# Gated linear attention with a bilinear feed-forward: scores of a 128-token block taken by its first and last 64 tokens, and a new order of all steps

## The chip, the cores and the metric

The kernel runs on one core of one Trainium2 chip. The metric is the time of one execution in microseconds on the device; the median of three runs of the kernel before is 193.85 us (193.69 to 193.97). The engines are called as in the profile: PE (TensorE, with its weight loads as PEld), DVE (VectorE), ACT (ScalarE), POOL (GpSimd) and SP (SyncE, which here only issues DMAs).

## The reference

There are 4 batch rows, 8 heads, 768 tokens and a head width of 48. Per batch row and head a 48 x 48 state is decayed row by row, updated and read:

```
for t in range(S):
    state = alpha[:, :, t, :, None] * state + einsum('bhd,bhe->bhde', k[:, :, t], v[:, :, t])
    y[:, :, t] = einsum('bhd,bhde->bhe', q[:, :, t], state)
x = y.transpose(0, 2, 1, 3).reshape(3072, 384)
out = ((x @ w_a) * (x @ w_b)) @ w_out        # w_a, w_b: 384 x 1536, w_out: 1536 x 384
```

## The kernel before

**Tiling.** The work is cut into six chunks, c = 0 to 5. A chunk is two batch rows (u = 0, 1; even c take rows 0 and 1, odd c rows 2 and 3) times 256 tokens. The 256 tokens lie on 128 partitions as pairs (r = 0, 1 within the pair), and the partitions fall into two halves of 64 (g = 0, 1); a half is a block of 128 consecutive tokens. Within a block the recurrence is worked out as masked scores between keys and queries; from block to block it goes through the state.

**The steps of one chunk**, with the short names that the program uses:

- `ld` loads alpha (a), k, q and v; `ln` (L556, ACT) takes logarithms of alpha; `B`, `A2` or `AQ` (PE) form running sums; `E` (L667, ACT) takes exponentials i and b of them; `ra`, `lv` scale one token of each pair; `mk`, `mq` (L678, DVE) write the scaled keys and queries into `QKp`, with heads padded from 48 to 64 columns.
- `C` (L736, PE) transposes `QKp` with eight 128 x 128 transposes per half of the heads, and `Ce` (L742, L744) copies the result from PSUM to `kqT`. That is so for chunks 0 and 1; for chunks 2 to 5 `T` (L767) is a DMA transpose issued by SP.
- `v` (L785, L787) copies the loaded values into `vx`, whose heads are padded with zeros from 48 to 96 columns (`cz .. v P`, L513, a POOL memset).
- `D` (L841, PE) forms scores, one call per u and half h of the heads: 16 matmuls of a 64 x 64 quarter of the array, each with 128 columns (the block's queries, both r). A stationary operand holds the block's 64 keys of one r. The result, 128 x 1024, is masked on its way out of PSUM by DVE (`M`, L846), or copied by ACT (`Mc`, L850) and masked in place by DVE (`Mm`, L854).
- `K` and `K2` (L799, L812, PE) form the state's updates, `k` (L826 to L830, DVE) applies them; `SB`, `SA` (PE, L865) are the parts of the output that come from the state, `Y` (PE, L865) is the part from the scores: 48 quarter matmuls with 128 columns per u. `X` (L900, L902) copies the output to `xT`.
- The feed-forward: `a f w` and `b f w` (L919, PE) are three matmuls each for the 128 columns f of w_a or w_b, with 512 columns of tokens (w = *) or 256 (one u); `as` (L925, ACT) copies a's result, `pr` (L933, DVE) multiplies; `o` (L941) and `oc` (L952) are the last product, `ot` and `otc` (L956, L958) copy it, `st` and `stc` store it (SP; one by ACT).

**The order** is written out by hand in a string `PROGRAM`: each entry is one step with its engine (V is DVE, S is ACT, P is POOL, Y is SP) and its PSUM bank. No planner runs when the kernel is built; each engine takes its instructions in the order of the string and waits for the semaphores of what it reads and overwrites. So an entry has two meanings: its place among the entries of its own engine, and its data. Between engines the string sets nothing. The weight loads `W a lo hi`, `W b lo hi` (L529) and `Wo` (L532) cast from float32 to bf16 and are issued by POOL, among POOL's own work.

PSUM has eight banks; a `D` and a `Y` take two, the other steps one.

Of the kernel before, what the change touches and what calls it, by code (L numbers as in the profile page):

```python
# [82 lines left out]
0: cs 1 0 P; o 3 1 -
1: k 0 0 V; k 0 1 V; Mm 0 0 V; SB 0 1; C 1 0 3; C 1 1 7
0: ot 3 S; o 0 1 -
1: Ce 1 0 V
2: ln *
1: v 1 V; D 1 0 3; Ce 1 1 S; K2 1 1 6 0; Y 0; SA 0
0: ot 0 V
1: k 1 0 V; D 1 1 6  # L90
0: o 2 0 5
1: M 1 0
2: l2 0 V
1: X 0 S; a 3 0 1; Mc 1 1
2: l2s 0 P; l2s 1 P
1: a 2 0 3; a 4 0 4
2: R 0
1: k 1 1 V; as 4 0
2: ra 1
1: as 3 0; b 4 0 7  # L100
0: o 2 1 -
1: as 2 0
0: ot 2 S
1: pr 4 0
2: R 1; lv 1 q P
1: b 3 0 6; b 2 0 7; a 5 0 2; pr 3 0; b 5 0 3; as 5 0; b 1 0 5; a 1 0 1; pr 5 0; pr 2 0; a 7 0 2; as 1 0; pr 1 0
2: AQ 3
1: SB 1 6
2: lv 0 k P
1: a 10 0 5  # L110
2: lv 1 k V; ra 0; ld v * P
1: Mm 1 1 V
2: E 1 b
1: as 10 0; b 10 0 0; pr 10 0
2: mq 1 V; E 1 i
1: as 7 0; b 7 0 1
2: E 0 b; E 0 i
1: a 0 0 5
0: st 3 Y
2: dr  # L120
1: SA 1; Y 1
2: mk 1 V
1: pr 7 0; a 11 0 0; a 6 0 3; b 6 0 2; X 1 S; b 11 0 4; a 2 1 6; as 6 0; a 3 1 7; as 11 0; b 2 1 1; pr 6 0
2: lv 0 q V
1: b 4 1 0; as 2 1
2: T 1
1: pr 11 0
2: dl
0: st 0 Y
1: a 0 1 2; pr 2 1  # L130
2: mq 0 V
1: b 3 1 3; b 0 0 6; as 3 1; as 0 0; b 0 1 7; pr 3 1; a 8 0 1; a 9 0 5
0: st 1 Y
1: b 8 0 3; b 9 0 4; pr 0 0; as 0 1
2: mk 0 V
1: a 4 1 2
3: ln *
1: a 9 1 6; pr 0 1; as 8 0; b 9 1 1
3: ra 1
1: b 10 1 7; pr 8 0; a 10 1 3; as 4 1; as 9 0; as 9 1; a 6 1 6; b 6 1 2; b 11 1 5; pr 4 1; as 10 1; pr 9 0; a 11 1 4; pr 10 1; pr 9 1; as 6 1  # L140
2: v 1 S
1: a 8 1 3; b 8 1 1; a 7 1 6; pr 6 1
3: l2 0 V
1: as 11 1
2: T 0
1: as 8 1; a 5 1 4
3: ra 0
1: as 5 1; a 1 1 2
2: v 0 V
4: ld a * Y  # L150
1: pr 11 1; as 7 1; pr 8 1
2: K2 * * 0 7; D 1 1 3; D 1 0 5
1: as 1 1; b 5 1 2; o 2 0 1
2: k * 0 V
1: pr 5 1
3: v 0 S; v 1 S
1: b 1 1 2
2: Mc 1 0; M 1 1
3: l2s 0 P; l2s 1 P
1: b 7 1 0; o 2 1 -; pr 1 1; o 3 0 4  # L160
2: SB 0 5
1: pr 7 1
3: R 0
2: D 0 0 2
1: ot 2 V
2: Mm 1 0 V
1: o 3 1 -
2: Mc 0 0; SB 1 0; D 0 1 2
3: R 1
1: ot 3 S  # L170
2: SA 0
1: o 0 0 4
0: cs 0 0 P
2: Mc 0 1
4: ln *
3: ld q * Y; ld k * Y
2: k * 1 V
3: AQ 2
2: Y 1; SA 1; Mm 0 1 V; Mm 0 0 V; Y 0; X 0 S
3: E 0 b  # L180
4: l2 0 V
2: X 1 V
1: o 0 1 -
2: b 1 * 6; a 1 * 5
3: E 1 b
4: ld k * Y
3: E 1 i
1: ot 0 S
3: E 0 i
4: l2s 0 P  # L190
2: a 0 * 0; b 0 * 1; as 0 *; as 1 *
3: lv 0 k P; lv 0 q P
2: a 5 * 7
1: st 3 Y
2: a 7 * 4
4: l2s 1 P
2: a 2 * 5
3: lv 1 q V; mq 1 V; lv 1 k V
2: pr 1 *
3: dr  # L200
2: pr 0 *
3: mk 0 V
4: ld q * Y
0: st 2 Y
2: as 5 *; a 6 * 6; b 6 * 2; as 7 *
3: mq 0 V
2: b 9 * 4; b 7 * 0
1: st 2 Y
3: dl
4: R 0  # L210
2: b 5 * 7
1: o 1 0 3
2: a 9 * 1; pr 7 *; as 6 *
3: T 0
2: pr 6 *
4: ra 0
# [188 lines left out]
def kernel(  # L405
# [11 lines left out]
    nc = tc.nc  # L417
# [148 lines left out]
    def bank(i):  # L566
        return psum[:, int(i)]
# [531 lines left out]
```

## Time and profile before

| | |
|---|---|
| median of three runs | 193.85 us |
| the profiled execution, first to last instruction (its span) | 192.0 us |
| that leaves around the span, against the median | 1.85 us |
| PE busy (matmuls as the profile models them) | 186.8 us |
| DVE busy | 133.1 us, 223 instructions |
| ACT busy | 106.5 us, 194 instructions |
| POOL busy | 56.9 us, 75 instructions |
| granted TensorE clock, mean | 1.000 |

The profile is one execution. Its chain of work that ended last is followed back from the last instruction: at each step to what released it, or to the instruction before it on its engine. Its time line lists instructions with their start, their duration and, in brackets, the idle time of the engine before them and what ended it. Matmuls overlap, so the duration of one says less than the distance between the starts of two.

### The profile page before, as it was taken

What the parts mean: (1) busy time and instruction counts of PE and PEld (TensorE: products, weight loads), DVE (VectorE), ACT (ScalarE), POOL (GpSimd) and SP (SyncE); (2) the same over time, 40 slices, a digit from 0 to 9 for tenths busy, and PEclk for the clock granted to TensorE, in tenths of its full rate; (3) what the DMA queues carried; (4) which work ended last, traced back from release to release, by engine and by line L of the source; (5) the groups of instructions that cost most, each with busy time, mean ns of one, the idle gap of its engine ahead of it and who ended that gap; (6) DMA issues with size and microseconds to landing.
All of it is one profiled execution on the core that took longest, in us unless ns stands there. A gap on an engine that the chain in (4) does not pass through costs nothing.

```text
span 192.0 us, 6086 instructions
## 1 busy us (share of the span) xinstructions
PE 186.8 (97%) x2613; PEld 116.9 (61%) x2613; DVE 133.1 (69%) x223; ACT 106.5 (55%) x194; POOL 56.9 (30%) x75
## 2 busy tenths in 40 slices
PE   7999999999999999999999999999999999999992
PEld 3888875677778876645557444656465644545562
DVE  2387698994989888899897956887567446252510
ACT  4448885656779867753487756743572435314211
POOL 8999626752450500640074262000000000000000
PEclk9999999999999999999999999999999999999999
DMA  5999999999969999999999989017641200000422
GB/s 132 274 219 218 251 253 235 244 269 264 251 107 166 165 216 265 248 254 149 233 213 181 156 174 129 3 42 140 146 66 44 85 0 0 0 0 3 164 82 82
DMA packets 62618, 29.40 MB, mean 153 GB/s; under 512 B 53712, under 2 KB 60768, under 8 KB 62592
## 3 DMA queue, kind: packets, MB, share of 16 engines
q0 software_dynamic: 18432, 13.37, 39.6%
q1 hardware_dynamic: 44016, 15.55, 38.1%
q8 instruction: 20, 0.33, 0.7%
q10 hardware_dynamic: 144, 0.10, 0.2%
q14 instruction: 6, 0.05, 0.1%
HBM read 25.98 MB, written 4.74 MB: 160 GB/s over the span
## 4 chain that ended last, share of the span: by engine, by line
PE 91%; DMA 5%; SPq 1%; DVE 1%; issue 1%; ACT 0%; DVEq 0%
PE psum L919 47%; PE psum L941 24%; PE psum L865 7%; PE psum L841 3%; DMA kqT<-QKp 3%; DMA q_t<-in_q_dram 3%; PE psum L736 2%; PE psum L633 1%; PE psum L952 1%; SPq L549 1%; PE psum L799 1%; PE psum L812 1%; PE psum L700 1%; PE psum L591 1%; PE psum L592 1%
## 5 line engine op out<-in xcount | busy, mean ns | idle before, releaser
L919 PE MATMUL psum<-xT,wb_t 128*128 128x512 bf16 (+1 forms) x270 | 56.0, 337 | 0.0
L919 PE MATMUL psum<-xT,wa_t 128*128 128x512 bf16 (+1 forms) x270 | 56.0, 337 | 0.0
L941 PE MATMUL psum<-wo_t,prod 128*128 128x384 bf16 x276 | 49.4, 326 | 0.0
L919 PEld LDWEIGHTS <-wb_t 128*128 128x128 bf16 x270 | 25.9, 98 | 19.9 <-issue 0.5
L919 PEld LDWEIGHTS <-wa_t 128*128 128x128 bf16 x270 | 25.9, 98 | 19.7 <-issue 0.3
L941 PEld LDWEIGHTS <-prod 128*128 128x128 bf16 x276 | 25.9, 98 | 17.6
L956 ACT ACTIVATE ot<-psum 128x384 f32<-128x384 f32 (+1 forms) x16 | 7.7, 482 | 22.7 <-PE psum L941 21.6
L850 ACT ACTIVATE m<-psum 128x1024 bf16<-128x1024 f32 x14 | 14.1, 1023 | 4.6 <-PE psum L841 4.3
L613 POOL TENSOR_TENSOR l<-la 64x384 f32<-64x384 f32 x7 | 7.8, 1108 | 26.6 <-ACT la L556 19.0
L846 DVE TENSOR_TENSOR m<-psum,mask 128x1024 bf16<-128x1024 f32 x10 | 12.1, 1220 | 3.1 <-PE psum L841 3.1
L652 POOL TENSOR_TENSOR q_t<-q_t,ra 128x384 f32<-128x384 f32 x5 | 6.1, 1215 | 22.5 <-ACT ra L645 19.7
L556 ACT ACTIVATE la<-a_t 128x1536 f32<-128x1536 f32 (+2 forms) x9 | 9.5, 1055 | 2.3 <-DMA a_t<-in_alpha_dram 2.2
L678 DVE TENSOR_TENSOR QKp<-q_t,beta 128x768 bf16<-128x768 f32 x10 | 10.0, 995 | 1.0 <-ACT beta L667 1.0
L865 PE MATMUL psum<-m,vx 64*64 64x128 bf16 x576 | 10.5, 217 | 0.0
L900 ACT ACTIVATE xT<-psum 128x768 bf16<-128x768 f32 x9 | 7.2, 816 | 5.7 <-PE psum L865 5.5
L678 DVE TENSOR_TENSOR QKp<-k_t,invb 128x768 bf16<-128x768 f32 x10 | 9.7, 972 | 0.8 <-ACT invb L667 0.8
L854 DVE TENSOR_TENSOR m<-m,mask 128x1024 bf16<-128x1024 bf16 x14 | 9.3, 684 | 1.2 <-ACT m L850 1.2
L958 DVE COPY ot<-psum 128x384 f32<-128x384 f32 (+1 forms) x9 | 4.8, 532 | 7.6 <-PE psum L941 4.7
L865 PEld LDWEIGHTS <-vx 64*64 64x64 bf16 x576 | 9.0, 107 | 0.5 <-issue 0.3
L841 PE MATMUL psum<-kqT 64*64 64x128 bf16 x384 | 9.0, 219 | 0.4 <-DMA kqT<-QKp 0.3
L652 POOL TENSOR_TENSOR k_t<-k_t,a_t 128x384 f32<-128x384 f32 x6 | 7.4, 1228 | 6.1 <-issue 3.3
L549 POOL DMA_DIRECT2D v_t<-in_v_dram x8 | 8.5, 1058 | 0.1
(271 smaller groups left out, 287.9 us busy)
## 6 DMA issues: line engine op xcount, KB each, us to landing
out_dram<-ot SPq DMA_DIRECT2D x23, 192.0 KB, 3.8
q_t<-in_q_dram SPq DMA_DIRECT2D x3, 768.0 KB, 6.5
a_t<-in_alpha_dram POOLq DMA_DIRECT2D x2, 768.0 KB, 15.2
k_t<-in_k_dram POOLq DMA_DIRECT2D x2, 768.0 KB, 12.1
v_t<-in_v_dram POOLq DMA_DIRECT2D x4, 384.0 KB, 7.0
a_t<-in_alpha_dram SPq DMA_DIRECT2D x2, 768.0 KB
k_t<-in_k_dram SPq DMA_DIRECT2D x2, 768.0 KB
a_t<-in_alpha_dram POOLq DMA_DIRECT2D x3, 384.0 KB, 8.5
```

What stands on the lines that cost most here:

```text
L549: eng.dma_start(out=t[:, us, hs].rearrange("p b h r d -> p (b h) (r d)"), in_=src[ch.b0 + us.start:ch.b0 + us.stop, hs, ch.s * 2 * C:(ch.s ...
L556: nc.scalar.activation(out=ch.la[:, us, hs].rearrange("p b h r d -> p (b h r d)"), in_=ch.a[:, us, hs].rearrange("p b h r d -> p (b h r d) ...
L613: eng.tensor_add(ch.l2[(1 - g) * HC:(2 - g) * HC, 1], x[:, :, 0, :], x[:, :, 1, :])
L652: eng.tensor_mul(x, x, by)
L678: eng.tensor_mul(QKp[ch.c % 2][:, u, j, :, hs, :D], src[:, u, hs].rearrange("p h r d -> p r h d"), f)
L841: nc.tensor.matmul(s2[g * HC:(g + 1) * HC, r, p, rk, :], lhsT=turned_part(ch, u, 1, rk, 2 * h + p, g, rs), rhs=queriesT(ch, u, 2 * h + p, ...
L846: nc.vector.tensor_mul(m.rearrange("p r a k s -> p (r a) (k s)"), ch.s2[u, h].rearrange("p r a k s -> p (r a) (k s)"), maskn(4))
L850: nc.scalar.activation(out=m.rearrange("p r a k s -> p (r a) (k s)"), in_=ch.s2[u, h].rearrange("p r a k s -> p (r a) (k s)"), func=AF.Copy)
L854: eng.tensor_mul(x, x, maskn(4))
L865: nc.tensor.matmul(y[c * DP:(c + 1) * DP, g, j // 2 * C:(j // 2 + 1) * C], lhsT=lhsT, rhs=rhs, start=(g, c) not in begun, stop=False, skip ...
L919: nc.tensor.matmul(p, lhsT=(wa_t, wb_t)[w][:, kk, f * 128:(f + 1) * 128], rhs=ch.xT[:, kk, us, :], start=(kk == 0), stop=(kk == KT - 1))
L941: nc.tensor.matmul(op, lhsT=ch.prod[:, f, at:at + C], rhs=wo_t[:, f, :], start=(f == 0), stop=(f == NFF - 1))
```

## The change

A block's 128 tokens were split by r: a stationary operand held the 64 tokens of one r. Now they are split into the first 64 tokens (x = 0) and the last 64 (x = 1). The last 64 keys are read only with the last 64 queries, so their score matmul has 64 columns and not 128, and likewise the `Y` matmul of x = 1. The scores of a call are 128 x 768 and not 128 x 1024, and the mask is 192 columns wide and not 256.

For this the keys of one x must lie together. In chunks 0 and 1 the transposes write PSUM in that order. In chunks 2 to 5, after the DMA transpose, a new step `Tr` copies the key half of `kqT` (128 x 1024, bf16) into a new tile `kp`: eight calls, five on DVE and three on ACT. The values must lie likewise: `v` copies them as before, and a new step `vs` then overwrites two of four quarters of 32 partitions in `vx` with the tokens of the other r (two instructions of 32 partitions x 384 each): 24 calls, 11 on DVE, 6 on ACT, 7 on POOL. `K` and `K2` read the loaded values and no longer `vx`.

The PROGRAM string is new from end to end. The steps of each kind are as many as before. What else stands on other engines than before: `Ce` six on ACT and two on DVE (before two and six), `v` four on ACT and eight on DVE (nine and three), `lv` seven on POOL and 13 on DVE (11 and nine), `l2s` four and four (seven and one), `l2` two on POOL and four on DVE (none and six).

The first lines of the string, before and after (up to the place where the feed-forward begins):

```diff
-0: cm 0; c1; cz 0 b P; ci; ld a 0b Y; c1a; ld a 0a Y; ln 0b; cu; cz 1 b P; fill 7 2; cu2 V; cz 0 q V; cus; ld k 0b Y; ld k 0a Y; B 0b 5; ld q 0b Y; ld v 0 P
-0: ln 0a; ld q 0a Y; E 0b b; E 0b i; mq 0b V; B 0a 0; E 0a i; dk 0 2; E 0a b; ld a 1 P; mk 0b V; C 0 1 5; cs 0 m P; ld k 1 P; ld q 1 P; v 0 S; mk 0a V; cm 1
-0: de 0; fill 2 1; mq 0a V; C 0 0 3; Ce 0 1 V; W b 0 256; cz 0 v P; Ce 0 0 V; D 0 1 4; ln 1; ld v 1 P; W a 256 768; K 0 0 6; k 0 0 V; M 0 1; D 0 0 0; SB 0 6
-0: cz 1 q P; B 1a 2; M 0 0; W a 0 256; E 1a i; E 1a b; W b 256 768; mq 1a V; mk 1a V; B 1b 4; dk 1 3; E 1b i; E 1b b; de 1; v 1 S; mq 1b V; mk 1b V; C 1 0 0
-0: Y 0; SA 0; Ce 1 0 V; cs 1 m P
+0: cm 0; c1; cz 0 b P; ci; ld a 0b Y; c1a; ld a 0a Y; ln 0b; cu; cz 1 b P; fill 7 0; cu2 V; cz 0 q V; cus; ld k 0b Y; ld k 0a Y; B 0b 2; ld q 0b Y
+0: ln 0a; B 0a 0; E 0b i; mk 0b V; ld v 0 P; fill 2 4; E 0b b; mq 0b V; C 0 1 2; ld q 0a Y; E 0a b; mq 0a V; dk 0 3; E 0a i; mk 0a V; ld a 1 P; C 0 0 0; Ce 0 0 V
+0: cs 0 m P; Ce 0 1 S; D 0 1 4; K 0 0 2; D 0 0 0; de 0; ln 1; ld k 1 P; v 0 S; k 0 0 V; SB 0 2; ld q 1 P; cm 1; M 0 0; vs 0 0 S; vs 0 1 P; W b 0 256; M 0 1
+0: B 1a 6; E 1a b; mq 1a V; B 1b 0; dk 1 4; E 1a i; mk 1a V; E 1b b; C 1 0 5; E 1b i; mq 1b V; cz 0 v P; Y 0; ld v 1 P; SA 0; mk 1b V; K 1 1 0; v 1 V
+0: vs 1 0 V; vs 1 1 V; de 1; K 1 0 1; k 1 0 V; C 1 1 4; Ce 1 1 V; Ce 1 0 S; D 1 0 6; X 0 S; W a 256 768; a 3 0 1; a 4 0 2; Mc 1 0; cz 1 q P; Mm 1 0 V; SB 1 4; as 4 0
+0: W a 0 256; as 3 0; D 1 1 6; a 0 0 3; k 1 1 V; Mc 1 1; Mm 1 1 V; a 5 0 2; a 1 0 1; as 1 0; b 1 0 0; pr 1 0; W b 256 768; b 4 0 6; pr 4 0; cs 1 m P; SA 1; b 3 0 1
...
```

and the core of the code (HQ is 32, HC is 64, C is 128):

```diff
+    def turn_keys(ch, u, eng):
+        t = alloc_t(ch, u)
+        x = wk.tile([C, 8 * C], BF16, name="kp", bufs=3)
+        ch.kp[u] = x.rearrange("p (h a q w) -> p h a q w", h=2, a=2, q=4)
+        ch.qT[u] = t[:, :8 * C].rearrange("p (r h a s) -> p h a r s", h=2, a=2, r=2)
+        evict(x.rearrange("p (y r s) -> p y r s", r=2, s=HQ), t[:, 8 * C:].rearrange("p (r y s) -> p y r s", r=2, s=HQ), eng)
...
+    def vswap(ch, us, g, eng):
+        for x in range(2):
+            to, of = (slice(g * HC + n * HQ, g * HC + (n + 1) * HQ) for n in (x, 1 - x))
+            o_ = vxs[ch.c % 2][to, us, 1 - x, :, :D]
+            i_ = ch.v[of, us, :, x, :]
...
+            evict(o_, i_, eng)
...
     def scores(ch, u, h, tag):
-            for rk in range(2):
+            for x in range(2):
                 for g in range(2):
                     for r in range(2):
                         rs = slice(r * DP, (r + 1) * DP)
-                        nc.tensor.matmul(s2[g * HC:(g + 1) * HC, r, p, rk, :], lhsT=turned_part(ch, u, 1, rk, 2 * h + p, g, rs),
-                                         rhs=queriesT(ch, u, 2 * h + p, g, rs), start=True, stop=True)
+                        nc.tensor.matmul(s2[g * HC:(g + 1) * HC, r, p, cols(x)], lhsT=keysT(ch, u, 2 * h + p, g, rs, x),
+                                         rhs=queriesT(ch, u, 2 * h + p, g, rs, x), start=True, stop=True)
...
     def inner(ch, u):
-                        out_mm(ch, u, g, h, j, vx[gs, u, rk, at:at + DP], ch.m[u, h // 4][gs, h % 2, h // 2 % 2, rk, :])
+                        m = ch.m[u, h // 4][gs, h % 2 * 2 + h // 2 % 2, cols(x)].rearrange("p (r s) -> p r s", r=2)
+                        out_mm(ch, u, g, h, j, vx[gs, u, x, at:at + DP], m, x)
```

Here `cols(0)` is 128 columns and `cols(1)` 64. `evict` is the copy that `ot` uses: an activation on ACT, a tensor copy on DVE or POOL.

More of the change, by code (lines that the diff above doesn't have):

```diff
@@ L116 @@
[L116 to L119, printed above, removed]
-2: dr
[L121 to L125, printed above, removed]
+0: o 0 0 3
+1: C 1 0 7
+0: cs 1 0 P
+1: SA 0; Mm 0 0 V; Y 0; X 0 S
+0: o 1 0 2; o 0 1 -
+1: v 1 V; vs 1 0 V
+2: ra 1
+1: vs 1 1 S; b 1 0 0
+2: l2s 0 V; l2 0 V
+1: a 2 0 1; Ce 1 0 S; a 1 0 4
+2: l2s 1 V; R 0
+0: ot 0 S
+1: a 4 0 5; as 4 0
+2: lv 1 q V; R 1
+1: as 1 0; pr 1 0; as 2 0
@@ new lines @@
+0: o 1 1 -; ot 1 S
+1: K2 1 1 7 3; k 1 0 V; D 1 1 4; Mc 1 1
+0: o 2 1 -; ot 2 S
+2: ra 0
+1: k 1 1 V; b 2 0 0; b 4 0 1; D 1 0 2
+2: lv 0 k V
+1: pr 2 0
+2: AQ 4
+1: SB 1 6
+2: E 0 i
+1: pr 4 0; M 1 0
+2: E 1 b
+1: a 5 0 0; as 5 0; a 7 0 1; as 7 0; b 5 0 2
+2: lv 0 q P
+1: a 10 0 3; a 6 0 0; SA 1
+2: lv 1 k V
+1: Mm 1 1 V
+2: ld v * P
+1: Y 1; pr 5 0
+2: E 0 b; mk 0 V; E 1 i
+1: as 6 0
+2: mk 1 V; mq 1 V
+1: a 3 0 2; b 10 0 0; as 10 0; pr 10 0; X 1 S; b 7 0 3
+2: dr
+3: ln *
+1: b 6 0 1; pr 6 0; pr 7 0; a 3 1 4
@@ L172 @@
-1: o 0 0 4
-0: cs 0 0 P
[L174 to L180, printed above, removed]
-4: l2 0 V
-2: X 1 V
+2: v 1 S
+1: a 8 0 3; a 5 1 0
+2: mq 0 V
+1: as 5 1
+2: vs 1 0 V
+1: pr 5 1; b 10 1 1; as 10 1; pr 10 1
+2: T 0
+1: a 0 1 6
+0: st 0 Y
+1: a 9 0 7; as 9 0
+4: ld a * Y
+2: vs 1 1 V
+1: b 9 0 0; pr 9 0
+3: ra 0
+1: b 2 1 4; as 8 0; b 8 0 5; pr 8 0; a 9 1 7
+2: v 0 V
+1: as 0 1; a 6 1 1; as 2 1
+2: K2 * * 0 3
+1: as 6 1
+3: ld q * Y
@@ new lines @@
+1: pr 8 1
+2: SB 1 4
+3: vs 1 0 S
+2: D 0 1 6; Mc 0 1
+3: vs 1 1 S; l2s 0 P; l2s 1 P; R 0
+1: o 3 0 2; o 3 1 -
+4: ln *
+3: R 1; AQ 6; E 0 b
+4: ld k * Y
+3: E 1 b
+2: SA 0; Mm 1 0 V; Y 1
+0: cs 0 0 P
+2: Mm 0 1 V; Mm 0 0 V; Y 0
+1: ot 3 V; st 3 Y
+3: E 1 i
+2: SA 1; X 1 V
+4: l2s 0 P
+1: o 1 0 2; o 1 1 -
+3: dr
+2: X 0 S; b 5 * 7; a 11 * 0; a 3 * 1
+4: ld q * Y
+3: lv 1 q P; lv 1 k V; mk 1 V
+2: as 3 *
+3: mq 1 V
+2: a 5 * 4; as 5 *; a 4 * 5
+3: lv 0 k V; lv 0 q V; mq 0 V
+4: ra 1
+3: E 0 i
+2: as 11 *
@@ new lines @@
+1: st 1 Y
+4: E 0 b; mq 0 V
+3: X 1 S; X 0 V; a 0 * 2
+4: E 0 i; mk 0 V
+3: a 6 * 3
+4: vs 0 1 S
+3: a 1 * 6
+4: E 1 i; T 0
+3: as 1 *; as 0 *
+2: ot 1 S
+5: l2 0 V; ld k * P; l2s 1 V
+3: b 1 * 4
+5: l2s 0 V
+3: a 11 * 5
+4: mk 1 V
+3: as 11 *
+4: v 1 V; mq 1 V
+3: b 2 * 6; b 6 * 0
+5: R 0
+3: pr 1 *
+4: vs 1 0 V; vs 1 1 V
+5: lv 0 k V
+3: b 0 * 2; pr 0 *; b 11 * 7; pr 11 *; as 6 *; pr 6 *; a 5 * 4; as 5 *; a 2 * 3; as 2 *
+2: o 0 1 -
+3: b 5 * 7
+4: Tr 0 V
+3: a 9 * 0; pr 2 *
+5: R 1; lv 1 q V
@@ new lines @@
+2: o 3 0 6; o 3 1 -
+4: k * 0 V; Tr 1 V
+3: as 3 *; pr 3 *
+4: SB 1 0
+5: E 0 b
+4: D 1 0 2
+2: ot 3 V
+4: Mc 1 0
+5: ld v * P
+4: D 0 1 4; M 0 1
+3: a 4 * 7; as 4 *
+5: lv 1 k V; mk 1 V
+2: st 3 Y
+3: a 7 * 6; as 7 *
+4: SB 0 2; D 1 1 4
+5: mk 0 V; dr
+3: a 10 * 7; b 4 * 6
+4: Mc 1 1; Mm 1 1 V; Mm 1 0 V
+3: b 7 * 4
+4: Y 0; SA 0; X 0 S
+5: lv 0 q V
+4: Y 1; SA 1
+3: b 10 * 5
+4: X 1 S
+3: as 10 *; pr 4 *; o 0 0 2
+4: a 9 * 3; b 4 * 0; a 0 * 1; a 4 * 6
+3: pr 7 *
+5: mq 0 V; T 0
+4: a 8 * 4; as 0 *; b 0 * 1; a 7 * 7
```

622 lines of the change are left out of this document (232 added, 390 removed).

## The prediction

> **What bounds the kernel now.** I read the page's busy times first, then the chain of waits, then the time lines of the first 25 us engine by engine.
>
> ```profile
> PE 186.8 (97%) x2613; PEld 116.9 (61%) x2613; DVE 133.1 (69%) x223; ACT 106.5 (55%) x194; POOL 56.9 (30%) x75
> ...
> PE 91%; DMA 5%; SPq 1%; DVE 1%; issue 1%; ACT 0%; DVEq 0%
> ```
>
> PE is busy from about 9 us to 188.7 us nearly without a break, and the chain runs through PE for 91% of the span. So a microsecond of PE work taken out is a microsecond of time, if PE is still fed; and a microsecond of new idle time on PE is a microsecond lost. The rest of the page does not bind on average, but DVE is close (36.3 of the 40 us from 60 to 100).
>
> The feeding at the start is the narrow place. Three time lines show it (POOL, then ACT, then PE):
>
> ```profile
> 8.50 0.77 POOL L529 DMA_DIRECT2D wb_t<-in_moe_w_b_dram  x1
> ...
> 9.99 0.90 POOL L549 DMA_DIRECT2D v_t<-in_v_dram  x1
> 10.88 0.75 POOL L529 DMA_DIRECT2D wa_t<-in_moe_w_a_dram  x1
> ```
>
> ```profile
> 9.28 0.84 ACT L785 ACTIVATE vx<-v_t 128x768 bf16<-128x768 bf16 x1 [0.42 <-DMA v_t<-in_v_dram]
> ...
> 10.80 0.84 ACT L556 ACTIVATE la<-a_t 128x768 f32<-128x768 f32 x1 [0.43 <-DMA a_t<-in_alpha_dram]
> ```
>
> ```profile
> 16.91 0.34 PE L865 MATMUL psum<-kqT,Sm 64*64 64x128 bf16 x6
> ...
> 18.32 0.50 PE L919 MATMUL psum<-xT,wa_t 128*128 128x256 bf16 x3
> ```
>
> POOL issues `W b 0 256` at 8.5, `ld v 1` at 10.0, `W a 256 768` at 10.9. The DMA issues of 8 to 16 us give 5.5 us to landing for that v and 6.5 for that w_a: they land at 15.5 and 17.4, and PE's first feed-forward matmul starts at 18.3. The weights come 0.9 us before they are needed.
>
> **PE work removed.** Half of the 384 score matmuls and half of the 576 `Y` matmuls go from 128 to 64 columns. The chain of waits gives rows for whole groups:
>
> ```profile
> 67.40 0.63 PE psum L812 x64
> ...
> 72.79 0.22 PE psum L841 x16
> 73.01 1.08 PE psum L941 x6
> ...
> 129.08 1.80 PE psum L865 x120
> ```
>
> A score matmul costs 0.22/16 = 13.8 ns, a `Y` matmul 1.80/120 = 15.0 ns, and a 64 x 64 quarter with 48 columns (L812) 9.8 ns; the other short group of L812, 0.25 us for 32, gives 7.8 ns. 64 columns lie between 48 and 128. Floor for the new cost 7.8: saving 192 x 6.0 + 288 x 7.2 = 3.2 us. With 9.8: 192 x 4.0 + 288 x 5.2 = 2.3. I take **-2.7 us**; the outer ends are 0 (the stationary loads bind and nothing is saved) and -3.2. On the Trainium skill, page "TensorE: Matmul & The Clock Gate", section "LDWEIGHTS (loading the stationary operand)": it gives P / 1.2 ns for P columns, so 53 ns for 64 of them. Four quarters at 4 x 13.8 = 55 ns would by that be held by their loads, and narrowing would save nothing; L812 loads the same 64 columns and runs four quarters in 31 to 39 ns, so the trace speaks against it here.
>
> **More changes between whole array and quarters.** In the chain six `o` matmuls take 0.98 us before another whole-array group and 1.08 before a quarter group (L941 at 73.01 above), so entering costs 0.1 us, and I estimate the same for leaving. I counted the runs of quarter steps (`K`, `D`, `SB`, `SA`, `Y`, `AQ`) in both strings: 25 before, 27 after. Two more at 0.2: **+0.4 us** (0 to +0.8).
>
> **Work beside PE.** Masks shrink by a quarter (`M` 1220 ns, `Mm` 684, `Mc` 1023 on the page, so about -0.27, -0.13, -0.21 each), `vs` and `Tr` come in. On DVE: 10 x -0.27, 14 x -0.13, five more `v` at 0.35, four fewer `Ce` at 0.69, 22 `vs` instructions at some 0.25 (half of `v`'s 0.35 and an overhead), five `Tr` between 0.35 and 0.69, four more `lv` at 0.55 to 0.75, one net `l2`/`l2s` at 0.55: together about +5, so 138 of 192. ACT: 14 x -0.21, five fewer `v` at 0.85, four more `Ce` at 1.02, 12 `vs` at 0.5, three `Tr` at 1.02: about +6, so 112. POOL about 61. None is a bound on average, so these go at nothing. What hides them is feed-forward on PE. For `Tr`, which stands between the DMA transpose (4.3 to 5.9 us to landing) and `D`, the tightest place is chunk 3, u = 0: between it and `D 0 1` stand one `o` half, one `b` and `K2`, 2.3 us of PE, and if the copy waits, DVE waits with it; uncovered it costs 1 us. The string holds about 23.8 us of DVE work against 20.0 of PE from chunk 0's last `o 0 1` to chunk 1's `a 4 1`, but 6.2 against 9.6 just ahead, so only part of the excess can show: 0 to +2, at nothing in the sum.
>
> **A step moved in front of the weight loads.** In the new string POOL has `vs 0 1 P` between `cm 1` and `W b 0 256`. POOL takes its entries in order, and behind `vs` wait `W b 0 256`, `cz 0 v`, `ld v 1`, `W a 256 768`, `W a 0 256`, `W b 256 768` and the loads of chunk 1. `vs 0 1` overwrites what `v 0 S` wrote, and ACT has `Ce 0 1 S`, `de 0`, `ln 1` ahead of `v 0 S` now. `ln 1` cannot start before 10.8 (the a_t row above), so `v 0` runs to 10.8 + 0.8 + 0.8 = 12.4 at the earliest; before it ended at 10.1. Then two POOL copies of 384 elements: no row has that form. The zero fill of 128 x 768 took 747 ns (half: 0.37), `l2s` with two inputs of 384 took 1108, a cast of 128 elements 281. I take 0.65 each, 1.3 for both (0.7 to 2.2). So:
>
> - `W b 0 256` is issued at 13.7 and not at 8.5; `cz 0 v` (0.75) follows its 0.8; `ld v 1` at 15.2, not 10.0; `W a 256 768` at 16.1, not 10.9.
> - By then the queue is dry: what was issued up to 7 us has landed by about 13.6 (6.2 + 7.5). A load that meets an idle queue is in the trace once:
>
> ```profile
> v_t<-in_v_dram POOLq DMA_DIRECT2D x1, 384.0 KB, 5.9
> ```
>
> That is the load issued at 54.3, and the windows show 3 us of movement in it. For 192 KB I take 5.9 - 1.5 = 4.4 (3.0 to 5.5). `v 1` lands at 19.6 (18.2 to 20.7).
>
> - PE now has `K 1 1` directly behind `Y 0` and `SA 0`, and `K 1 1` reads that v. Before, `SA 0` ended near 17.0 with 17.2 for the next step; the same work with a shorter `Y` and small gains ahead brings PE there at 16.6. **New idle 3.0 us** (1.5 to 4.1).
> - `K 1 1`, `K 1 0`, `C 1 1` and `D 1 0` take 0.25 + 0.25 + 0.55 + 0.2: PE is at `a 3 0` at 20.9. `W a 256 768` lands 5.2 after 16.1 (between 4.4 and 6.5), 21.3: **0.4 more**. `W b 256 768`, issued near 18.2, lands near 23.7 and is wanted at 23.9. Chunk 1's loads come later by as much as PE is late.
>
> In sum +3.4 (1.5 to 6). The start itself is a little better: `mk 0b`, which needs no q, now stands ahead of `mq 0b`, and the first transposes no longer wait for both behind the q load; but `D 0 0` still waits for a copy out of PSUM: **-0.3** (-0.6 to 0).
>
> The Trainium skill, page "DMA: Bandwidth & Descriptors", section "Anatomy of one DMA — SWDGE (gpsimd) path", fits a POOL-issued DMA as 2.0 us plus bytes / 436e3. For 192 KB that is 2.5 us, `v 1` would land at 17.7, the new idle time would be 1.1 and not 3.0, and the sum below 1.9 lower. The load at 54.3 would by it take 2.9 us and took 5.9, so I do not go by it; it is part of the first rival.
>
> **Tail.** Both orders end with twelve half-width `oc` matmuls, a 0.33 us copy and a store: nothing, 0 to +0.3, since the last store is now SP's behind another.
>
> **Sum**, against the execution's own span: 192.0 - 2.7 + 0.4 + 3.4 - 0.3 = 192.8. The median stands 1.85 us above the span: **194.6 us**. For this kernel a measurement can tell some 0.2%, 0.4 us, from no change.
>
> **Rivals.**
>
> 1. *Not slower: the late loads reach PE in time.* Then 192.0 - 2.7 + 0.4 - 0.3 = 189.4, with 0.5 to 1.5 us of idle time 189.9 to 190.9, so 191.3 to 192.8 measured; its centre 191.9. For it: before, PE had nearly no stall in 180 us, and DMA that is not queued lands sooner than under load. Against it: the 5.9 us row, and that PE has no other work between `SA 0` and `a 3 0`. The point from which it decides is the landing of `v 1`: before 17.8 the kernel is faster.
> 2. *DVE binds in chunks 1 and 2.* The excess above shows on top of the forecast: +1.8, 196.4. For it: DVE already had 36.3 of 40 us. Against it: its work ahead is light.
> 3. *Narrow matmuls save nothing.* +2.7: 197.3. The L812 rows speak against it.
>
> **Chances.** Forecast 0.52 (its own range 193.2 to 196.0), rival 1 0.30, rival 2 0.12, rival 3 0.06. Of the forecast 0.10 fall within 0.2%, 0.04 below; of rival 1, 0.03 within 0.2% and the rest below. So faster 0.31, the same 0.13, slower 0.56. The range reaches from the middle of rival 1's span to rival 3's time, with the bounds of the copies and the landing in it: 191.3 to 197.3; some 0.15 is left out.
>
> **What the changed kernel's profile would show.** `W b 0 256` on POOL near 13.7 behind the two copies, `ld v 1` near 15.2; PE idle for about 3 us before `K 1 1`, released by the v load; the DMA rate near nothing between 13.6 and 15; score and `Y` matmuls of 64 columns, with the sum of PE's time between 24 us and the end shorter by 2.3 us. Wrong it would be if POOL's copies run before 12 us (then `v 0` did not wait for `ln 1`), if `v 1` lands before 17.8, if the narrow matmuls stand as far apart as the wide ones, or if PE idles after 40 us for DVE.

## The result and the profile after

| | before | after |
|---|---|---|
| median | 193.91 us (193.69 to 194.69) | 207.5 us (205.71 to 208.95) |
| profiled execution | span 192.0 us | span 206.1 us, time 207.83 us |
| mean granted TensorE clock | 1.000 | 0.967 |

After over before is 1.0658, 95% interval 1.0606 to 1.071. Forecast were 194.6 us, at most 197.3: the direction was right, the size was not. Times here and below are medians of all runs, while a ratio to the kernel before, and its interval, holds only the fast runs (within 1.5% of their kernel's fastest), so differences between kernels are taken from the ratios, times 193.9 us. The busy times, the granted clock and the chain of waits of the changed kernel's page:

```profile
PE 189.6 (92%) x2613; PEld 116.8 (57%) x2613; DVE 139.7 (68%) x256; ACT 111.1 (54%) x208; POOL 55.8 (27%) x84
...
PEclk9999589999999999999999759999999999999999
...
PE 67%; DMA 20%; POOL 4%; DVE 3%; ACT 2%; issue 1%; SPq 1%; POOLq 0%; ACTq 0%
```

PE falls from 97% to 92% of a longer span, the chain leaves it for DMA in a fifth of the span, and twice the clock is cut (slices 5 to 6 and 23 to 24). The forecast knew one of the places. Its time lines, POOL and then PE (start, duration, instruction, and in brackets the idle time ahead with its releaser):

```profile
12.33 1.05 POOL L939 COPY vx<-v_t 32x384 bf16<-32x384 bf16 x2 [3.71 <-ACT vx L748]
13.33 0.77 POOL L506 DMA_DIRECT2D wb_t<-in_moe_w_b_dram  x1
...
14.82 0.90 POOL L526 DMA_DIRECT2D v_t<-in_v_dram  x1
15.71 0.75 POOL L506 DMA_DIRECT2D wa_t<-in_moe_w_a_dram  x1
```

```profile
18.71 0.59 PE L771 MATMUL psum<-v_t,QKp 64*64 64x48 bf16 x32 [1.48 <-DMA v_t<-in_v_dram]
...
22.79 1.46 PE L900 MATMUL psum<-xT,wa_t 128*128 128x256 bf16 x6 [2.64 <-DMA wa_t<-in_moe_w_a_dram]
```

POOL waits for ACT's cast of v, and the three loads go out within 0.4 us of the forecast (13.7, 15.2, 16.1). PE is idle for 4.1 us there, 3.4 were forecast. The second place was not forecast at all. The chain of waits between 98 and 121 us (start, length, what):

```profile
98.44 0.76 SPq L955
...
99.77 15.05 DMA a_t<-in_alpha_dram
...
114.91 1.49 ACT la L533
...
116.91 0.48 ACT ot L937
...
117.43 4.00 PE psum L922 x12
```

SP issues chunk 5's alpha (`5: ld a * Y`) behind two transposes and two stores (the row of L955 is the first store); it lands 15 us later; ACT stands at `5: ln *`, and behind that in ACT's order is `2: ot 2 S`, which frees the bank that PE's next step writes. The waits of PE have it as the largest of all:

```profile
PE psum L922 <- ACT ot L937: 5.1, 1, 5.1
```

In the kernel before, the logarithm of chunk 5 stood ahead of `ot 2 S` in ACT's order as well. But there SP issued the load right behind the two transposes, ahead of the stores and 8 us ahead of POOL's next loads of v and k, and ACT reached the logarithm without idle time (SP's row, then ACT's, of the kernel before):

```profile
91.25 0.96 SPq L549 DMA_DIRECT2D a_t<-in_alpha_dram  x1
...
99.14 1.48 ACT L556 ACTIVATE la<-a_t 128x1536 f32<-128x1536 f32 x1
```

So it is the load that lost its place in the new order, not the logarithm.

Then the 12 matmuls of L922 take 4.00 us, 333 ns each. The same form takes 162 ns each at 195 us:

```profile
195.19 1.95 PE psum L922 x12
```

Windows show why (busy time of the five engines, PEclk, DMA share, GB/s; this is the changed kernel):

```profile
20.00:24.00 4.00, 1.36 (x22) 0.74 (x10) 2.87 (x7) 0.81 (x1) 3.95 (x6) 0.53 1.24 221
24.00:28.00 4.00, 4.00 (x46) 2.76 (x44) 1.00 (x3) 2.37 (x5) 2.71 (x4) 0.62 1.09 241
...
112.00:117.00 5.00, 0.38 (x32) 0.31 (x17) 0.00 (x0) 2.00 (x3) 0.00 (x0) 0.88 0.83 186
117.00:122.00 5.00, 4.57 (x14) 2.02 (x14) 3.40 (x5) 4.16 (x10) 0.00 (x0) 0.50 0.22 81
```

The granted clock is 0.50 from 20.2 to 27.1 us and from 115.8 to 122.6 us. So PE, busy again after each stall, runs at half rate for another 4 to 5 us.

What was forecast as a gain came. In the chain, 16 score matmuls and the 120 matmuls of `Y`, `SA` in one stretch:

```profile
80.88 0.17 PE psum L816 x16
...
142.63 1.51 PE psum L845 x120
```

Before they took 0.22 and 1.80. That is 24 x 0.05 and 6 x 0.29 us, 2.9 us in all. The account of the 14.1 us by which the two spans differ: PE's idle time 12.1 us against 0.55 (the sum of the gaps between matmuls that exceed 0.1 us), +11.5; half rate behind the two stalls, 16 matmuls at 213 ns for 109 and 15 at twice their time, 1.6 + 2.7, +4.3; narrow matmuls -2.9; two more changes of array mode +0.4, as forecast, which no run measured; 0.8 is left over.

### The profile page after: what moved, and what is told of

Same layout as the page of the kernel before. It is cut to its first block, busy times and chain, and to the rows that moved or that the text cites. A ratio compares the mean times of both kernels' runs of the same rounds, so it can differ in the third digit from the quotient of the medians.

```text
span 206.1 us, 6122 instructions
## 1 busy us (share of the span) xinstructions
PE 189.6 (92%) x2613; PEld 116.8 (57%) x2613; DVE 139.7 (68%) x256; ACT 111.1 (54%) x208; POOL 55.8 (27%) x84
## 4 chain that ended last, share of the span: by engine, by line
PE 67%; DMA 20%; POOL 4%; DVE 3%; ACT 2%; issue 1%; SPq 1%; POOLq 0%; ACTq 0%
PE psum L900 36%; PE psum L922 22%; DMA a_t<-in_alpha_dram 14%; DMA wo_t<-in_moe_w_out_dram 6%; PE psum L845 4%; PE psum L816 2%; ACT la L533 1%; PE psum L933 1%; PE psum L715 1%; POOL v_t L526 1%; PE psum L610 1%; POOL wb_t L506 1%; POOL wa_t L506 1%; DVE k_t L629 1%; DVE prod L914 1%
## 5 line engine op out<-in xcount | busy, mean ns | idle before, releaser
L900 PE MATMUL psum<-xT,wa_t 128*128 128x512 bf16 (+1 forms) x270 | 57.5, 348 | 2.6 <-DMA wa_t<-in_moe_w_a_dram 2.6
L922 PE MATMUL psum<-wo_t,prod 128*128 128x384 bf16 x276 | 51.0, 335 | 5.1 <-ACT ot L937 5.1
L922 PEld LDWEIGHTS <-prod 128*128 128x128 bf16 x276 | 26.9, 100 | 24.3 <-issue 6.8
L939 POOL COPY vx<-v_t 32x384 bf16<-32x384 bf16 x14 | 7.0, 502 | 71.0 <-ACT vx L748 53.4
L829 ACT ACTIVATE m<-psum 128x768 bf16<-128x768 f32 x14 | 11.2, 811 | 8.3 <-PE psum L816 8.0
L937 ACT ACTIVATE ot<-psum 128x384 f32<-128x384 f32 (+1 forms) x16 | 7.8, 485 | 13.7 <-PE psum L922 13.2
L825 DVE TENSOR_TENSOR m<-psum,mask 128x768 bf16<-128x768 f32 x10 | 9.4, 950 | 2.0 <-PE psum L816 1.1
L833 DVE TENSOR_TENSOR m<-m,mask 128x768 bf16<-128x768 bf16 x14 | 7.3, 550 | 3.0 <-ACT m L829 3.0
L845 PE MATMUL psum<-m,vx 64*64 64x128 bf16 (+1 forms) x576 | 8.6, 205 | 0.4 <-issue 0.4
L845 PEld LDWEIGHTS <-vx 64*64 64x64 bf16 x576 | 7.5, 108 | 1.4 <-issue 1.1
L845 PE MATMUL psum<-kqT,Sm 64*64 64x128 bf16 x144 | 8.0, 224 | 0.0
L845 PEld LDWEIGHTS <-Sm 64*64 64x64 bf16 x144 | 5.0, 108 | 3.3 <-issue 2.6
## 6 DMA issues: line engine op xcount, KB each, us to landing
out_dram<-ot SPq DMA_DIRECT2D x23, 192.0 KB, 2.2
a_t<-in_alpha_dram POOLq DMA_DIRECT2D x2, 768.0 KB, 12.1
```

The lines of the kernel that those rows point to most:

```text
L825: nc.vector.tensor_mul(m, x, maskn())
L829: nc.scalar.activation(out=m, in_=x, func=AF.Copy)
L833: eng.tensor_mul(m, m, maskn())
L845: nc.tensor.matmul(o, lhsT=lhsT, rhs=rhs, start=(g, c) not in begun, stop=False, skip_group_check=True)
L900: nc.tensor.matmul(p, lhsT=(wa_t, wb_t)[w][:, kk, f * 128:(f + 1) * 128], rhs=ch.xT[:, kk, us, :], start=(kk == 0), stop=(kk == KT - 1))
L922: nc.tensor.matmul(op, lhsT=ch.prod[:, f, at:at + C], rhs=wo_t[:, f, :], start=(f == 0), stop=(f == NFF - 1))
```

## The experiments

The theory after the traces: the new order is not short of engine time; it leaves waits in which an in-order queue stands at an operand that comes late, PE is idle behind it, and after that it runs at half rate. The rivals: the late loads bind wherever they are waited for; an engine binds and each repair shows the next wait; the half rate has another cause.

**1. The loads ahead of the copy.**

```diff
-vs 0 0 S; vs 0 1 P; W b 0 256; M 0 1
+vs 0 0 S; W b 0 256; cz 0 v P; ld v 1 P; W a 256 768; vs 0 1 P; M 0 1
```

> The changed kernel with one edit: on POOL, the first w_b load, the zero fill of vx, the v load of sequences 1 and the first w_a load are issued ahead of the copy that swaps values, and not behind it. Theory (PE is idle for late loads, and runs at half rate after it): the idle time of 1.48 and 2.64 us at 17 and 20 us goes, and with it the 15 feed-forward matmuls that stand 213 ns apart and not 110 (1.6 us): 207.5 - 5.7 = 201.8 us, granted clock of the window 10 to 38 us near 1.00, the stall at 112 us as it was. Rival (the loads were late for the DMA's sake, not POOL's): they land no earlier than 18 us for v, idle time stays above 2 us, 205 us or more.

203.77 us (ratio 1.0479, 1.0413 to 1.0544), 3.5 us faster than the changed kernel, where 5.7 were expected. Of the two stalls at 17 and 20 us, 0.31 and 0.47 us are left; idle time at 38 us rose from 1.6 to 2.2 us. The clock was not near 1.00 throughout: in experiment 3, which has this edit too, it was 0.50 from 11.1 to 14.5 us and, behind the idle time at 38 us, from 41.8 to 45.2 us.

**2. ACT's logarithm later,** and **3. both.**

```diff
-5: ld a * Y; ln *; ra 0
+5: ld a * Y
...
-5: ra 1
...
-5: l2 0 V; ld k * P
+5: ln *; ra 0; ra 1; l2 0 V; ld k * P
```

> The changed kernel with one edit: on ACT, the logarithm and the two exponentials of chunk 5's alpha go behind the last output copies of chunk 2, the load stays where it is. Theory (ACT stood at the logarithm, and the output copy that frees PE's bank was queued behind it): idle time of 5.05 us at 112 us goes, with the half rate behind it (2.6 us): 207.5 - 7.6 = 199.9 us. Rival 1 (the load itself is what PE needs): the wait moves to DVE and to the cumulated sums of chunk 5, 205 us or more. Rival 2 (half rate has another cause than the idle time): 202.4 us, and the clock still falls near 117 us.

> Both edits of the two kernels before, the rest of the change as it is. Theory (these two places hold the whole loss): 207.5 - 5.7 - 7.6 = 194.2 us, mean granted clock 0.99 or more. Rival (a repaired wait lets another one bind, on DVE or on the alpha load): 197 us or more, and PE's idle time is then found elsewhere.

205.59 us (1.0615, 1.0567 to 1.0662) and 204.31 us (1.0526, 1.0493 to 1.0559): a miss, both: the second edit alone brought 0.8 us of 7.6, and with the first one in it brought nothing. DVE and then PE of the kernel with both edits:

```profile
116.35 0.56 DVE L540 TENSOR_TENSOR l<-la 128x384 f32<-128x384 f32 x1 [4.84 <-ACT la L532]
...
120.96 0.72 DVE L913 TENSOR_TENSOR prod<-as__2371,psum 128x512 bf16<-128x512 bf16 x1
```

```profile
121.73 2.72 PE L899 MATMUL psum<-xT,wa_t 128*128 128x512 bf16 x6 [4.60 <-DVE prod L913]
```

The same alpha now stops DVE at its next reader, and behind it in DVE's order is the product that frees PE's bank. The stall changed its queue: the first rival of experiment 2 was right about where it goes.

**4. PE kept busy in the stalls,** to part half rate from idle time.

```diff
-K 1 1 0;
+fill 6 0; K 1 1 0;
...
-a 3 0 1; a 4 0 2
+fill 11 1; a 3 0 1; a 4 0 2
...
-2: o 1 0 0; o 1 1 -
+3: X 0 V; fill 22 4
+2: o 1 0 0; o 1 1 -
...
-3: X 1 S; X 0 V; a 0 * 2
+3: X 1 S; a 0 * 2
```

> The changed kernel with both stalls left in, but PE kept busy in them by matmuls on zeros into a free bank (6 ahead of the state product at 17 us, 11 ahead of the first feed-forward step, 22 ahead of the output step at 112 us; for the last, one copy out of PSUM on DVE stands ahead of a product that waits). Theory (the half rate follows from PE's idle time): the clock stays at 1.00, the stalls keep their length, 207.5 - 1.6 - 2.6 = 203.3 us. Rival (the half rate comes from the work or the moment, not from idle time): clock falls as before, 207.5 us or more.

206.01 us (1.0615, 1.0565 to 1.0665). Two of the windows above, of this kernel:

```profile
20.00:24.00 4.00, 2.94 (x35) 1.61 (x34) 3.38 (x9) 0.81 (x1) 3.95 (x7) 1.00 1.25 188
...
117.00:122.00 5.00, 5.00 (x27) 2.44 (x25) 4.82 (x8) 4.14 (x9) 0.00 (x0) 1.00 0.55 125
```

In this trace the clock stays at 1.00 throughout, with the waits left in: the half rate behind these two stalls follows from PE's idle time. (The other three runs have a mean clock of 0.987 to 0.992, against 0.967 in the changed kernel.) The time fell by 0.8 us, with intervals that overlap, and not by 4.2; the fills themselves held PE up, for `a 3 0` begins at 24.2 and not 22.8, and `o 1 0` half a microsecond behind its release.

**5. DVE's readers later as well.** To experiment 3:

```diff
-5: ln *; ra 0; ra 1; l2 0 V; ld k * P; l2s 1 V
+5: ln *; ra 0; ra 1; ld k * P
...
-5: l2s 0 V
...
-5: R 0
 3: pr 1 *
 4: vs 1 0 V; vs 1 1 V
-5: lv 0 k V
-3: b 0 * 2; pr 0 *; b 11 * 7; pr 11 *;
+3: b 0 * 2; pr 0 *
+5: l2 0 V; l2s 1 V; l2s 0 V
+3: b 11 * 7; pr 11 *
+5: R 0; lv 0 k V
```

> The kernel with both edits (204.3 us) and one more: on DVE, the three pair sums of chunk 5 and what follows from them go behind chunk 4's products and casts and the feed-forward products that free PE's banks. In that kernel DVE stood 4.84 us for the logarithm of chunk 5, and PE 4.60 us for the product behind it. Theory (the wait for the late alpha stops whichever in-order queue its first reader stands in): PE's 4.60 us go, and the half rate behind them (some 2.5 us): 204.3 - 7.1 = 197.2 us. Rival (PE needs the alpha itself by then): the idle time moves to the cumulated sums of chunk 5 near 125 us, 201 us or more.

197.46 us (1.0192, 1.0131 to 1.0253): -6.5 us, 7.1 expected. The alpha lands as late as before (14.7 us after its issue), and PE does not need it by then.

**6. The alpha load earlier,** in place of its readers later. To experiment 1:

```diff
-5: ld a * Y; ln *; ra 0
+5: ln *; ra 0
...
+5: ld a * P
 4: l2s 1 P
```

> The kernel with the early weight loads (203.8 us) and one more edit: the load of chunk 5's alpha is issued by POOL near 93 us, ahead of the v and k loads of chunks 4 and 5, and not by SP at 98 us behind two transposes, two stores and those loads. All compute stays in its place. Theory (the alpha lands late, 14.4 us after its issue, because some 1.6 MB of other loads were issued just ahead): it lands by 102 us, ACT does not stop, 5.2 us of idle time and 2.5 us of half rate go: 196.1 us. Rival (the transfers are slow at this time for the transposes' sake): it lands after 106 us, and PE is still idle for 3 us or more.

202.59 us (1.0357, 1.0278 to 1.0436), 2.4 us below experiment 1, where 7.7 were expected: a miss. The alpha lands 8.4 us after its issue, at 99 us, as the theory had it, and ACT does not stop for it. But chunk 3's keys come late now. Experiment 8 below has the same edit; there the chain of waits reads:

```profile
85.57 8.96 DMA kqT<-QKp
...
95.03 0.54 PE psum L814 x13
```

The transpose (`3: T`) takes 8.96 us to landing. In experiment 7, without the early load, it was issued at 86.15 us and the copy that reads it started at 91.25, without a wait, so it took 5.1 us at most. The load gained 6.0 us against experiment 1 (14.4 to 8.4), the transpose lost at least 3.9, and PE was idle for 3.4 us before the scores that read it.

**7. The swap later on DVE.** To experiment 5:

```diff
-1: v 0 V
 0: a 9 * 2
-1: vs 0 0 V
...
-1: E 1 i; K2 0 0 5 6; C 0 1 7; vs 0 1 P
+1: E 1 i; K2 0 0 5 6; v 0 V; C 0 1 7; vs 0 0 V; vs 0 1 P
```

> As the kernel with the pair sums later, and one more edit: DVE's cast and swap of v for chunk 1 (36 to 40 us) go behind the inverse decay product and the state step. There the swap took 1.04 us an instruction and not 0.26, the cast 1.26 and not 0.35, while POOL worked, and PE was idle for 2.25 us. Theory (the swap stretches beside POOL and holds up the product behind it): idle time near 39 us under 0.5 us, no half rate behind it: 197.2 - 4 = 193.2 us. Rival (any DVE work there stretches as much): the product itself takes over 2 us, PE is idle for 1.5 us or more, 196 us.

DVE as it was in experiment 3, and PE behind it (in experiment 5 the cast took 0.68 us and the two swaps 2.07):

```profile
36.28 1.26 DVE L749 COPY vx<-v_t 128x768 bf16<-128x768 bf16 x1
37.57 2.08 DVE L938 COPY vx<-v_t 32x384 bf16<-32x384 bf16 x2
39.66 1.25 DVE L654 TENSOR_TENSOR QKp<-k_t,invb 128x768 bf16<-128x768 f32 x1
```

```profile
40.96 0.44 PE L783 MATMUL psum<-v_t,QKp 64*64 64x48 bf16 x32 [2.25 <-DVE QKp L654]
```

194.42 us (1.002, 0.9995 to 1.0045): -3.3 us, 4 expected. No idle time is left at 39 us. The product itself took 1.71 us in its new, earlier place:

```profile
34.80 1.71 DVE L650 TENSOR_TENSOR QKp<-k_t,invb 128x768 bf16<-128x768 f32 x1
```

So the rival was half right: this work stretches there too; it only no longer stands in PE's way.

**8. Alpha earlier and the swap later.**

> As the kernel with the alpha load on POOL, with the cast and swap of v for chunk 1 later on DVE as well. Theory (these are the places of the loss: the weight loads behind a copy, the swap beside POOL, the alpha load behind other loads): 196.1 - 4 = 192.1 us, within 1% of the kernel before and below it if no new wait shows. Rival (each repair lets another wait show): 196 us or more.

200.3 us (four runs, 197.47 to 202.71), where 192.1 were expected: a miss for the cause told under 6.

**9. Three more waits taken up.** To experiment 7: `v 1`, `vs 1 0` and `vs 1 1` of chunk 0 behind `k 1 0` and `Ce 1 1` on DVE; chunk 5's `ra` behind `as 5`, its `R 0` and `lv 0 k` behind `pr 6`.

> As the kernel with the pair sums and the swap later (194.4 us), with the last three idle stretches of PE above 0.5 us taken up: at 18 us (0.90) the cast and swaps of v 1 go behind the state product's two DVE steps and a copy that PE waits for; at 113 and 116 us (0.59 and 0.85) the exponentials and the residual of chunk 5 go behind the copies and products of feed-forward. Theory (the loss of the new order is the sum of such waits): 194.4 - 2.3 = 192.1 us, below the kernel before's 193.9. Rival (other waits show, or the alpha chain of chunk 5 is late for its sums): 194 us or more.

194.19 us (1.001, 0.9999 to 1.0022): nothing gained that can be told. PE's idle time fell from 4.0 to 3.5 us only: 0.93 us came back at 22 us, where the swaps now stood ahead of `k 1 1`, and 0.62 at 120 us, where DVE was without a pause; another 0.72 were at 9 us, where DVE stood at a load of q. Here the rival held.

**10. The narrow matmuls at full width.** To experiment 9:

```diff
-        return slice(x * C, C + x * HC)
+        return slice(x * C, C + x * C)
...
-                                         rhs=queriesT(ch, u, 2 * h + p, g, rs, x), start=True, stop=True)
+                                         rhs=queriesT(ch, u, 2 * h + p, g, rs), start=True, stop=True)
...
-                        m = ch.m[u, h // 4][gs, h % 2 * 2 + h // 2 % 2, cols(x)].rearrange("p (r s) -> p r s", r=2)
+                        m = ch.m[u, h // 4][gs, h % 2 * 2 + h // 2 % 2, cols(0)].rearrange("p (r s) -> p r s", r=2)
...
-                        out_mm(ch, u, g, h, j, vx[gs, u, x, at:at + DP], m, x)
+                        out_mm(ch, u, g, h, j, vx[gs, u, x, at:at + DP], m)
```

> As the tuned kernel, but the score matmuls of the last 64 tokens and the matmuls that take them up keep 128 columns (so these scores and sums are not the reference's). It prices the narrowing, forecast at 2.7 us: slower than the tuned kernel by 2.7 (2.3 to 3.2) us, 194.8 us. Rival (the stationary loads bind and narrow matmuls save nothing): the same as the tuned kernel, 192.1 us.

196.99 us (1.0168, 1.013 to 1.0206): the narrowing is worth 3.1 us, good to some 0.8, where 2.7 were forecast.

**11. The copy ahead of the loads again,** in the tuned kernel.

> As the tuned kernel, but POOL's copy stands ahead of the first loads of w_b, v 1 and w_a again, as in the changed kernel. It prices this one move, forecast at 3.4 us of idle time. Theory now: 3.4 to 4.1 us of idle time and 1.6 us of half rate, 5 to 5.7 us: 197.5 us, the clock at 0.5 for 4 to 6 us behind 20 us. Rival (the forecast was whole, no half rate): 195.5 us, clock 1.00.

198.16 us (1.0218, 1.0203 to 1.0234): the one move costs 4.0 us, 3.4 were forecast, 5 to 5.7 expected. Idle time behind 19 us was 2.3 us (0.43, 0.87 and 1.00), and in this trace the clock stayed at 1.00 there, against the expectation. The other three runs have a mean clock of 0.983 and not 0.991, which fits one more stretch at 0.50 of 3.4 us somewhere; where, no trace shows.

**12. The waits of experiment 9 taken up.** On DVE `mk 0a` ahead of `mq 0a` (and on ACT their exponentials likewise), `k 1 1` ahead of `v 1` and the swaps; `l2s` of chunk 5 on POOL.

> As the tuned kernel (194.2 us), with its remaining idle stretches of PE taken up: at 9 us (0.72) the product with k, which is there, goes ahead of the product with q, which is waited for; at 22 us (0.93) DVE's second state step goes ahead of the cast and swaps of v 1; at 115 and 119 us (0.30 and 0.62) two pair sums of chunk 5 go from DVE to POOL. Theory (the tuned kernel equals the kernel before only because 3.5 us of idle time against 0.55 eat the 2.8 us that the narrow matmuls save): 194.2 - 2.0 = 192.2 us, 0.9% below the kernel before. Rival (PE's work is no shorter in all, or each mended wait lets the next show): 194 us.

192.77 us (0.9914, 0.9881 to 0.9948), 0.9% below the kernel before and 14.4 us below the changed one, with the same work on every engine but for two sums moved from DVE to POOL:

```profile
PE 184.2 (96%) x2613; PEld 113.4 (59%) x2613; DVE 137.6 (72%) x254; ACT 110.8 (58%) x208; POOL 58.0 (30%) x86
...
PEclk9999999999999999999999999999999999999999
```

**13 and 14. POOL put to work beside DVE,** at a quiet place of experiment 12 (107 us): eight products, or four loads, that no result uses.

> The better tuned kernel, with 8 products on POOL (128 x 256, of zeros, into scratch; no result uses them) from the time that chunk 4's last exponential is there (some 107 us), beside DVE's cast, products and four swaps of v 1, which ran beside an idle POOL there: swap 0.26 us, cast 0.35, product 0.95. Theory (DVE's instructions that read and write SBUF alone stretch beside POOL's compute): swaps of 0.4 us and more, products of 1.1 or more, those that read PSUM as before (0.72). Rival (the stretch near 39 us came from something else, DMA traffic for one): all durations within 5% of those before.

> The better tuned kernel, with 4 small loads of alpha into scratch (98 KB each, not used) issued by POOL at the same place, in place of the products of the other kernel. Theory (DVE stretches while POOL writes out a load's descriptors, as well): the instructions beside the issues take 1.3 times their time or more. Rival (only POOL's compute does it): within 5%.

DVE without them (experiment 12), beside POOL's products, and beside POOL's issue of loads, whose two rows stand first:

```profile
108.63 0.35 DVE L746 COPY vx<-v_t 128x768 bf16<-128x768 bf16 x1
108.90 0.95 DVE L651 TENSOR_TENSOR QKp<-q_t,beta 128x768 bf16<-128x768 f32 x1
109.77 0.72 DVE L910 TENSOR_TENSOR prod<-as__2371,psum 128x512 bf16<-128x512 bf16 x1
110.52 1.05 DVE L935 COPY vx<-v_t 32x384 bf16<-32x384 bf16 x4
```

```profile
108.39 0.77 DVE L747 COPY vx<-v_t 128x768 bf16<-128x768 bf16 x1
109.08 1.37 DVE L652 TENSOR_TENSOR QKp<-q_t,beta 128x768 bf16<-128x768 f32 x1
110.37 0.73 DVE L911 TENSOR_TENSOR prod<-as__2381,psum 128x512 bf16<-128x512 bf16 x1
111.13 2.67 DVE L936 COPY vx<-v_t 32x384 bf16<-32x384 bf16 x4
```

```profile
108.88 2.88 POOL L982 DMA_DIRECT2D scr<-in_alpha_dram  x4 [0.35 <-POOL scr L980]
111.75 1.18 POOL L523 DMA_DIRECT2D k_t<-in_k_dram  x1
...
109.27 0.48 DVE L747 COPY vx<-v_t 128x768 bf16<-128x768 bf16 x1
109.67 0.94 DVE L652 TENSOR_TENSOR QKp<-q_t,beta 128x768 bf16<-128x768 f32 x1
...
111.29 1.73 DVE L936 COPY vx<-v_t 32x384 bf16<-32x384 bf16 x4
```

Beside POOL's products the copies take 2.2 to 2.5 times as long and the product of two SBUF tiles 1.4 times; the product that reads PSUM is as before. Beside the issue of the four small loads the cast takes 1.4 times as long and the product does not change. Of the four swaps three take 0.25 to 0.30 us, hardly more than without, the third of them already beside the issue of the 768 KB load of k; the fourth, from 112.13 us on, beside the rest of that issue, takes 0.88. That is near the 1.00 and 1.06 us of the swaps in experiment 3, which ran beside the issue of loads of v and q and a product on POOL. On the Trainium skill, page "SBUF — State Buffer", section "SBUF: two separate sides": DVE and GpSimd share one pair of ports, which one instruction holds to its end; a DVE copy in a fast mode needs it, and an instruction with two SBUF inputs only against a GpSimd instruction that reads SBUF. The three blocks agree with it, the unchanged product included. The product of experiment 7 does not: it took 1.71 us while POOL did nothing but issue loads (33.82 to 37.01 us). What stretched it is open. Both kernels came out at 201.5 and 203.2 us (one run each): POOL's extra work, ahead in its queue, also pushed back a load of k that chunk 5 waited for.

## Why the prediction was wrong

Step by step, as it was put:

- **"PE work removed", -2.7: right.** 2.9 by the chain's rows, 3.1 by experiment 10.
- **"A step moved in front of the weight loads", +3.4: right in mechanism, near in size.** 4.1 us idle in the trace, 3.5 by experiment 1, 4.0 by experiment 11. Its parts were off: POOL's two copies took 1.05 us (1.3 forecast), v came at 18.7 (19.6), the w_a load took 7.1 us and not 5.2. That 3.5 comes so near to 3.4 is luck in part: 4.1 us of idle time and 1.6 of half rate stood there, and the idle time that grew at 38 us took some of the gain back.
- **"None is a bound on average, so these go at nothing. What hides them is feed-forward on PE": this is the step that failed.** Feed-forward hides work that can be late; it does not hide an instruction that stands in an in-order queue ahead of one that frees a PSUM bank. The later place of chunk 5's `ld a` was not looked at, and `v` and `vs` were counted as busy time; what stands behind a moved step was followed for POOL's start and, in part, for `Tr` alone. What the runs showed in its place, half rate included: chunk 5's alpha 5.6 us (experiment 1 to 5), cast and swap ahead of the product 3.3 us (5 to 7), the shorter waits of 9 and 12 another 2.1 us. That is 11.0 of the 12.1 us by which the forecast was short (the ratio puts the changed kernel at 206.7 us); by the intervals each step is good to 0.8 to 1.7 us.
- **The rival "DVE binds in chunks 1 and 2", 1.8 us,** named the engine but not the cause: DVE's instructions ahead of that product stretched, which the sum of durations from quieter rows could not hold. In experiment 3 the cast and the swaps took some four times their length; in the changed kernel itself, where PE was idle for 1.6 us, the cast took 0.97 us and the product 1.22, against 0.35 and 0.95 in a quiet place:

```profile
41.24 0.97 DVE L750 COPY vx<-v_t 128x768 bf16<-128x768 bf16 x1
...
42.98 1.22 DVE L655 TENSOR_TENSOR QKp<-k_t,invb 128x768 bf16<-128x768 f32 x1
```

- **A term for the clock was missing.** The sum priced 3 us of idle time as 3 us. In the trace 4.3 us came on top of some 9, and experiment 4 shows that they come from the idle time. On the Trainium skill, page "TensorE: Matmul & The Clock Gate", section "What's actually happening": PE falls to half its clock after a window of some 3.4 us without work and needs such a window of work to come back. The traces agree on 0.50 and on windows of 3.4 us, and the second cut came 3.4 us into a stall; but the first came behind a window with only 1.5 us of idle time, so a window need not be wholly without work. It was a rule against this change, and should have been a rival.
- **Rival 1's lower end, 191.3, is its sum without any idle time** (189.4 + 1.85); with the 0.5 us that it names it is 191.8, and the range starts there at the lower end and not at the middle. Nothing hangs on it here.

Of the other 1.1 us, 0.1 are the first move's (3.5 for 3.4); 1.0 is what the best kernel here (192.2 by its ratio) stands above the forecast less its 3.4 us (191.2), and that kernel still has 2.8 us of idle time, 1.1 of them at 27 us.

Open is why the alpha takes 15 us to land. Its place in line counts: in the kernel before, ahead of the stores and of POOL's loads, it took 7.9 us at most (91.25 to 99.14), and 8.4 us in experiments 6 and 8, where the transposes pay for it; which of the loads, transposes and stores of 91 to 105 us hold each other was not parted.

## What to carry to other kernels

When a schedule is laid anew, an engine's busy share says little; follow each moved instruction through its queue, ask which operand it waits for and when that lands, and who needs what stands behind it. A load is such an instruction: here its issue had slid behind two stores. Late operands are best met by readers placed late in every queue (ACT's and DVE's here), since one reader moved only hands the stall to the next. And price idle time of PE at more than its length.

## What the runs showed of the hardware

- **The clock is set window by window.** In every trace here the stretches between two changes of the granted clock are multiples of 3.41 us (changed kernel: 13.65 us at 1.00, 6.83 at 0.50, 88.75 at 1.00, 6.83 at 0.50, 85.33 at 1.00), and this grid lies differently in each run. So runs of one kernel differ: experiment 7 has mean clocks from 0.991 to 1.000. From 15 us on, the clock fell at the end of windows of the grid with 1.55 us of PE's idle time and more (1.55 at 20.2 us and 3.41 at 115.8 us in the changed kernel, 1.98 at 21.9 us in experiment 2), and not with up to 1.3 us (1.23 at 44.1 us in the changed kernel, 1.12 at 26.6 us in experiment 11); some windows with 1.5 to 1.9 us did not do it either (1.90 at 120.8 us in experiment 2). In the first 13 us less was enough: 1.00 us in experiment 9 (at 11.1 us) and 0.41 in experiment 5 (at 11.8 us), though not 0.52 in experiment 8 (at 13.0 us). What else counts is open; much of the work there is small or f32 matmuls. A cut lasted 3.41 or 6.83 us.
- **POOL slows DVE by kind of instruction:** a swap from 0.26 to 0.67 us and a cast from 0.35 to 0.77 beside its products; 0.25 to 0.30 and 0.48 beside its issue of small loads, and 0.88 for a swap beside the issue of a 768 KB load; nothing for what reads PSUM (0.72 and 0.73).
